# Moving the first denominator sums and the output-weight folds, and loading the last turned w_mod blocks behind wo, in a TensorE-bound attention and SwiGLU block

## The chip, the cores and the metric

The kernel runs on one core of a Trainium2 chip. The metric is the device time of one execution in microseconds; lower is better. All kernels shown here gave correct results.

"PE" is the matrix engine TensorE, "PEld" its weight loads, "DVE" VectorE, "ACT" ScalarE, "POOL" GpSimd, "SP" the engine that issues most DMA transfers.

## The reference

One block with adaptive layer norm: a linear attention, then a SwiGLU feed-forward, both gated by rows of `silu(c) @ w_mod`. Sizes: 2048 tokens, D = 1024, 32 heads of 32, F = 3584, bf16.

```python
sa, ca, ga, sb, cb, gb = split(silu(c) @ w_mod)           # six rows of 1024
h = layernorm(x) * (1 + ca) + sa
q, k, v = h @ wqkv;  pq, pk = phi(q), phi(k)              # phi(t) = t+1 if t>0 else exp(t)
kv, z = pk^T v, sum(pk)                                   # per head, over all tokens
o = (pq @ kv) / (pq . z)
x = x + ga * (o @ wo)
h = layernorm(x) * (1 + cb) + sb
x = x + gb * ((silu(h @ w_gate) * (h @ w_up)) @ w_down)
```

## The kernel before

The tokens go through in four quarters (`sc` = 0 to 3) of 512. For each quarter the kernel computes K, then V; the KV sums of a quarter (`kv_phase`) are put between the first two K groups of the next quarter and the other six. After the last quarter come the queries of the other three quarters (those of the first are done earlier), 8 groups a quarter, with small work between the groups: two transposes, the denominator sums of the first quarter (`den_sum(0)`), and four "folds", which multiply ga * wo by the KV matrix of each head so that attention and output projection become one product. `hT` is the normed input of a quarter, transposed by DMA. The rows for the gates and norms need blocks of w_mod that are also transposed while they are loaded: these are the "turned w_mod blocks" (tiles `wmt`).

```python
    def kv_phase(sc):                        # 128 weight loads and 128 matmuls, 128x32 array tiles
        kvp = acc_b("kvp", (HG, 2, DH))
        for hg in range(HG):
            for t in range(STC):
                for i in range(HPC):
                    mm(kvp[i * DH:(i + 1) * DH, hg, :, :], lhsT=pks[sc][...], rhs=v_ones(vs[sc], ...), ...)
        ...
    for sc in range(NSC):
        if sc > 0:
            k_phase(sc, 0, 2)
            kv_phase(sc - 1)
            if sc == NSC - 1:
                wo = [big("wo", [4, D]) for _ in range(2)]
                for h in range(2):
                    for g in range(4):       # eight loads of 256 KB
                        with tc.issue_after(last_load[0].ins):
                            nc.sync.dma_start(out=wo[h][g * DH:(g + 1) * DH, :, :], in_=wo_v[h, g])
            k_phase(sc, 2, 8)
        v_phase(sc)
        ...                                  # layer norm of the next quarter, DVE sums for ga, sb, cb
        if sc + 1 < NSC:                     # two transposing loads of w_mod for a later row
            with tc.issue_after(last_load[0].ins):
                last_load[0] = mod_load(*((2, gaT), (3, sbT), (4, cbT))[sc])
    ...
    q_phase(1, 2, 4)
    tpk = acc_b("tp", (2, P), BF16)
    ...                                      # two transposes of KV
    den_sum(0)                               # 32 matmuls, 128x32 tiles; one acc_b bank
    den_spread(0)
    def fold_wo(h, nb):                      # 16 matmuls, 32x32 tiles; all four acc_b banks
        ps = [acc_b("wf") for _ in range(4)]
        ...                                  # then two casts on ACT, two on DVE
    q_phase(1, 4, 6)
    fold_wo(0, 0)
    q_phase(1, 6, 8)
    fold_wo(0, 1)
    q_phase(2, 0, 2)
    fold_wo(1, 0)
    q_phase(2, 2, 3)
    fold_wo(1, 1)
    ...
    q_phase(2, 3, 4)
    den_apply(0)                             # four DVE products
    q_phase(2, 4, 6)
    for st in range(STC):
        wo_tile(st)                          # output projection of the first quarter
```

`issue_after` only fixes the order in which one engine issues; it adds no wait.

## Time and profile before

| | kernel before |
|---|---|
| time, median of 6 runs | 834.01 us (833.39 to 834.51) |
| span in the trace | 831.7 us |
| granted TensorE clock | 1.0 |

Two lines of the page: busy time of each engine with its share of the span, and the chain of waits that ended last.

```profile
PE 820.7 (99%) x4502; PEld 379.3 (46%) x4581; DVE 344.8 (41%) x655; ACT 168.7 (20%) x253; POOL 64.4 (8%) x166
PE 98%; DVE 1%; issue 1%; ACT 0%; POOL 0%
```

Only TensorE counts: it is 98% of that chain. How long a piece costs it is best read on ScalarE: every query group ends in an exp, and nearly every exp starts when its group is finished (of ScalarE's 74.8 us of idle time before the 64 exps of K and query groups, 70.5 us ended with a matmul). This is the timeline of ScalarE in the kernel before (start, duration, instruction, and in brackets the idle time before it and what ended it).

```profile
146.99 0.60 ACT L295 ACTIVATE eb<-acc 128x512 bf16<-128x512 f32 x1 [1.14 <-DVE wo L557]
...
153.43 0.60 ACT L295 ACTIVATE eb<-acc 128x512 bf16<-128x512 f32 x1 [1.13 <-PE acc L98]
155.93 0.60 ACT L295 ACTIVATE eb<-acc 128x512 bf16<-128x512 f32 x1 [1.91 <-PE acc L98]
157.66 0.60 ACT L295 ACTIVATE eb<-acc 128x512 bf16<-128x512 f32 x1 [1.13 <-PE acc L98]
159.86 0.60 ACT L295 ACTIVATE eb<-acc 128x512 bf16<-128x512 f32 x1 [0.64 <-PE acc L98]
...
167.70 0.60 ACT L295 ACTIVATE eb<-acc 128x512 bf16<-128x512 f32 x1 [0.63 <-PE acc L98]
...
170.70 0.60 ACT L295 ACTIVATE eb<-acc 128x512 bf16<-128x512 f32 x1 [0.73 <-PE acc L98]
...
174.15 0.60 ACT L295 ACTIVATE eb<-acc 128x512 bf16<-128x512 f32 x1 [1.13 <-DVE pq L459]
```

A plain group is 1.73 us (155.93 to 157.66). Transposes and sums added 0.77 us (153.43 to 155.93), fold 1 0.47 us (157.66 to 159.86), but fold 4 added 1.27 us (167.70 to 170.70). The chain of waits says why (start, duration, what):

```profile
166.46 0.69 DVE pq L298
167.16 1.20 DVE wo L596 x2
168.36 0.04 issue
168.40 0.43 PE wf L98 x13
```

Fold 4 waited for VectorE to empty the banks of fold 3, only one query group earlier.

And the DMA queue's timeline there, first the turned w_mod blocks, then wo:

```profile
110.76 8.85 SPq L388 DMA_TRANSPOSE wmt<-in_w_mod_dram  x2
119.70 4.89 SPq L544 DMA_DIRECT2D wo<-in_A_wo_dram  x8
```

### The profile page before, as it was taken

How to read it: one execution, taken by the hardware profiler on the slowest of the kernel's cores; microseconds unless marked ns; L12 is line 12 of the kernel's file. 1: busy time of each engine (PE TensorE's matmuls, PEld its weight loads, DVE VectorE, ACT ScalarE, POOL GpSimd, SP SyncE). 2: the span in 40 equal slices, each digit the busy share in tenths (PEclk: the TensorE clock that was granted, in tenths of full speed). 3: DMA queues.
4: the chain of work that ended last, by engine and by line, in shares of the span. 5: the costliest groups of instructions: out<-in, count | busy, mean ns of one | idle time of the engine just before them, and what ended most of it. 6: DMA issues, size and time to landing. Idle time of an engine off the chain costs nothing.

```text
span 831.7 us, 11105 instructions
## 1 busy us (share of the span) xinstructions
PE 820.7 (99%) x4502; PEld 379.3 (46%) x4581; DVE 344.8 (41%) x655; ACT 168.7 (20%) x253; POOL 64.4 (8%) x166
## 2 busy tenths in 40 slices
PE   8999999999999999999999999999999999999998
PEld 4444444444444444444444444444444444444444
DVE  5757779896344335421111354211114431111122
ACT  3445343434111111101111110111111101111000
POOL 2101020110221101100000010000001100000000
PEclk9999999999999999999999999999999999999999
DMA  9793694229996635646343173753405529610011
GB/s 328 292 203 90 119 214 88 53 81 280 377 239 230 216 126 165 169 142 218 116 140 114 54 219 95 250 193 98 156 1 169 154 69 346 228 47 0 19 58 51
DMA packets 144100, 129.07 MB, mean 155 GB/s; under 512 B 58608, under 2 KB 124656, under 8 KB 143536
## 3 DMA queue, kind: packets, MB, share of 16 engines
q1 hardware_dynamic: 139968, 114.97, 46.5%
q0 software_dynamic: 3792, 12.98, 5.2%
q8 instruction: 36, 0.59, 0.3%
q10 hardware_dynamic: 288, 0.40, 0.1%
q14 instruction: 16, 0.13, 0.0%
HBM read 101.98 MB, written 12.72 MB: 138 GB/s over the span
## 4 chain that ended last, share of the span: by engine, by line
PE 98%; DVE 1%; issue 1%; ACT 0%; POOL 0%
PE acc L98 90%; PE a_ps L98 7%; PE kvp L98 1%; DVE stats L224 0%; PE mod_ps L98 0%; PE den L98 0%; ACT xn L234 0%; DVE wo L596 0%; PE tp L101 0%; PE wf L98 0%; DVE pq L298 0%; ACT eb L295 0%; POOL rstd L218 0%; DVE mv L225 0%; DVE veps L216 0%
## 5 line engine op out<-in xcount | busy, mean ns | idle before, releaser
L98 PE MATMUL acc<-h2T,wgu 128*128 128x512 bf16 x1756 | 385.7, 379 | 1.9
L98 PEld LDWEIGHTS <-wgu 128*128 128x128 bf16 x1792 | 175.3, 98 | 211.3
L665 DVE TENSOR_TENSOR gu<-acc,e 128x512 bf16<-128x512 f32 x112 | 77.4, 691 | 289.9 <-PE acc L98 278.8
L98 PE MATMUL acc<-wd,gu 128*128 128x512 bf16 (+2 forms) x908 | 195.2, 372 | 0.9
L664 ACT ACTIVATE e<-acc 128x512 f32<-128x512 f32 x112 | 66.9, 597 | 374.8 <-PE acc L98 363.4
L98 PEld LDWEIGHTS <-gu 128*128 128x128 bf16 x924 | 89.3, 98 | 104.5
L98 PEld LDWEIGHTS <-hT 128*128 128x128 bf16 x512 | 49.6, 98 | 59.9 <-issue 0.7
L686 DVE TENSOR_TENSOR e<-acc,gb_bc 128x512 f32<-128x512 f32 (+2 forms) x33 | 22.3, 675 | 131.7 <-PE acc L98 122.7
L98 PE MATMUL a_ps<-wo,pq 128*128 128x512 bf16 x250 | 56.9, 379 | 0.3
L98 PE MATMUL acc<-wk,hT 128*128 128x512 bf16 x251 | 56.3, 379 | 0.7 <-issue 0.5
L98 PE MATMUL acc<-hT,wq 128*128 128x512 bf16 x248 | 55.7, 379 | 0.8 <-issue 0.6
L98 PE MATMUL acc<-wv,hT 128*128 128x512 bf16 x249 | 55.5, 379 | 0.4
L295 ACT ACTIVATE eb<-acc 128x512 bf16<-128x512 f32 x64 | 37.9, 596 | 74.8 <-PE acc L98 70.5
L234 ACT ACTIVATE xn<-x,nmr,rstd 128x1024 bf16<-128x1024 f32 x16 | 19.8, 1240 | 126.0 <-POOL nmr L232 126.0
L633 POOL DMA_DIRECT2D x_scratch<-x x16 | 9.8, 615 | 378.2 <-DVE x L626 378.2
L98 PEld LDWEIGHTS <-pq 128*128 128x128 bf16 x256 | 25.1, 98 | 30.2
L98 PEld LDWEIGHTS <-wq 128*128 128x128 bf16 x256 | 24.6, 98 | 29.8 <-issue 0.9
L296 DVE TENSOR_SCALAR eb<-eb 128x512 bf16<-128x512 bf16 x64 | 18.4, 291 | 32.2 <-ACT eb L295 32.0
L218 POOL TENSOR_TENSOR rstd<-veps,neg_half 128x1 f32<-128x1 f32 x32 | 17.8, 556 | 102.5 <-DVE veps L216 90.9
L626 DVE TENSOR_TENSOR x<-a_ps,x_sb 128x512 f32<-128x512 f32 x32 | 22.1, 690 | 8.1 <-PE a_ps L98 7.4
L689 DVE TENSOR_TENSOR ob<-e,x1r 128x512 bf16<-128x512 f32 (+2 forms) x33 | 22.3, 675 | 1.0
L627 DVE BATCH_NORM_STATS2 stats<-x 128x6 f32<-128x512 f32 x32 | 22.2, 694 | 1.1
(88 smaller groups left out, 297.3 us busy)
## 6 DMA issues: line engine op xcount, KB each, us to landing
wgu<-in_B_w_gate_dram SPq DMA_DIRECT2D x28, 1024.0 KB, 7.9
wgu<-in_B_w_up_dram SPq DMA_DIRECT2D x28, 1024.0 KB, 8.3
x_sb<-in_A_x_dram SPq DMA_DIRECT2D x32, 256.0 KB, 5.8
x_scratch<-x POOLq DMA_DIRECT2D x16, 512.0 KB, 3.4
x1r<-x_scratch SPq DMA_DIRECT2D x31, 256.0 KB, 2.8
wd<-in_B_w_down_dram SPq DMA_DIRECT2D x7, 1024.0 KB, 6.2
rbc<-rden_scratch POOLq DMA_DIRECT2D x16, 256.0 KB, 7.3
out_dram<-ob SPq DMA_DIRECT2D x31, 128.0 KB, 1.7
```

What stands on the lines that cost most here:

```text
L98: return tc.keep_in_program_order(nc.tensor.matmul(out, lhsT=lhsT, rhs=rhs, start=start, stop=stop))
L218: nc.gpsimd.tensor_tensor(out=rstd[:, 0:n], in0=veps[:, 0:n], in1=neg_half[:].to_broadcast([P, n]), op=ALU.pow)
L234: nc.scalar.activation(out=dst, in_=src, func=ACT.Identity, bias=nmr[:], scale=rstd[:, 0:1])
L295: nc.scalar.activation(out=e[:], in_=acc, func=ACT.Exp)
L296: nc.vector.tensor_scalar(out=e[:], in0=e[:], scalar1=1.0, scalar2=PHI_EPS, op0=ALU.min, op1=ALU.add)
L626: nc.vector.tensor_tensor(out=x1[:, ns], in0=a_ps[:], in1=x_t[:, ns], op=ALU.add)
L627: nc.vector.bn_stats(out=stats[:, nb, :], in_=x1[:, ns])
L633: nc.gpsimd.dma_start(out=x1_dram[st * P:(st + 1) * P, :], in_=x1[:])
L664: nc.scalar.activation(out=sg[:], in_=ps[0][:], func=ACT.Silu)
L665: gm = nc.vector.tensor_tensor(out=guT[sc][f // GPT][:, f % GPT, :], in0=ps[1][:], in1=sg[:], op=ALU.mult)
L686: nc.vector.tensor_tensor(out=yt, in0=y_ps, in1=gb_bc[:, ns], op=ALU.mult)
L689: nc.vector.tensor_tensor(out=ob, in0=yt, in1=x1r, op=ALU.add)
```

## The change

It takes away the wait of fold 4 by keeping all folds two query groups apart, joins the denominator sums to fold 1 so that TensorE leaves its full-array shape once less, and puts wo ahead of the last turned w_mod blocks in the DMA queue. Cut to its core:

```diff
-    def den_sum(sc):
+    def den_sum(sc, den=None):
-        den = acc_b("den")
+        den = den or acc_b("den")
 ...                                            # in the loop over quarters, sc == NSC - 1
-                            nc.sync.dma_start(out=wo[h][...], in_=wo_v[h, g])
+                            last_load[0] = nc.sync.dma_start(out=wo[h][...], in_=wo_v[h, g])
+                with tc.issue_after(last_load[0].ins):
+                    mod_load(4, cbT)
             k_phase(sc, 2, 8)
 ...
-        if sc + 1 < NSC:
+        if sc + 2 < NSC:
             with tc.issue_after(last_load[0].ins):
-                last_load[0] = mod_load(*((2, gaT), (3, sbT), (4, cbT))[sc])
+                mod_load(*((2, gaT), (3, sbT))[sc])
 ...
     q_phase(1, 2, 4)
     ...                                        # two transposes
-    den_sum(0)
-    den_spread(0)
-    q_phase(1, 4, 6)
-    fold_wo(0, 0)
-    q_phase(1, 6, 8)
-    fold_wo(0, 1)
-    q_phase(2, 0, 2)
-    fold_wo(1, 0)
-    q_phase(2, 2, 3)
-    fold_wo(1, 1)
+    q_phase(1, 4, 5)
+    den_sum(0, acc_a())
+    fold_wo(0, 0)
+    den_spread(0)
+    q_phase(1, 5, 7)
+    fold_wo(0, 1)
+    q_phase(1, 7, 8)
+    q_phase(2, 0, 1)
+    fold_wo(1, 0)
+    q_phase(2, 1, 3)
+    fold_wo(1, 1)
 ...
-        den_apply(0)
-    q_phase(2, 4, 6)
+        applied = den_apply(0)
+    with tc.issue_after(applied.ins):
+        q_phase(2, 4, 6)
```

More of the change, by code (lines that the diff above doesn't have):

```diff
@@ L458, in den_apply @@
             ks = slice(2 * k, 2 * k + 2)
-            nc.vector.tensor_tensor(out=pq[:, ks, :], in0=pq[:, ks, :], in1=rbc[:, ks, :], op=ALU.mult)
+            last = nc.vector.tensor_tensor(out=pq[:, ks, :], in0=pq[:, ks, :], in1=rbc[:, ks, :], op=ALU.mult)
+        return last
     nc.vector.memset(sel[:], 0.0)
@@ L543 @@
                         with tc.issue_after(last_load[0].ins):
-                            nc.sync.dma_start(out=wo[h][g * DH:(g + 1) * DH, :, :], in_=wo_v[h, g])
+                            last_load[0] = nc.sync.dma_start(out=wo[h][g * DH:(g + 1) * DH, :, :], in_=wo_v[h, g])
+                with tc.issue_after(last_load[0].ins):
+                    mod_load(4, cbT)
             k_phase(sc, 2, 8)
@@ L578 @@
                             in1=zmask[:], op=ALU.mult)
-    q_phase(1, 2, 4)
-    tpk = acc_b("tp", (2, P), BF16)
-    for h in range(2):
-        transpose(tpk[:, h, :], KVB[:, 4 * h:4 * h + 4, :].rearrange("p g e -> p (g e)"))
-    nc.vector.tensor_copy(out=KVT, in_=tpk[:])
-    den_sum(0)
-    den_spread(0)
     def fold_wo(h, nb):
@@ L596, in fold_wo @@
             (nc.scalar.copy if g % 2 == 0 else nc.vector.tensor_copy)(out=wo[h][:, g, ns], in_=ps[g][:])
-    q_phase(1, 4, 6)
+    q_phase(1, 2, 4)
+    tpk = acc_b("tp", (2, P), BF16)
+    for h in range(2):
+        transpose(tpk[:, h, :], KVB[:, 4 * h:4 * h + 4, :].rearrange("p g e -> p (g e)"))
+    nc.vector.tensor_copy(out=KVT, in_=tpk[:])
+    q_phase(1, 4, 5)
+    den_sum(0, acc_a())
     fold_wo(0, 0)
-    q_phase(1, 6, 8)
+    den_spread(0)
+    q_phase(1, 5, 7)
     fold_wo(0, 1)
-    q_phase(2, 0, 2)
+    q_phase(1, 7, 8)
+    q_phase(2, 0, 1)
     fold_wo(1, 0)
-    q_phase(2, 2, 3)
+    q_phase(2, 1, 3)
     fold_wo(1, 1)
```

## The prediction

> **What bounds the kernel.** TensorE. On the page PE is busy 820.7 of 831.7 us (99%) at full granted clock, and the chain of waits is 98% PE. PE's waits sum to about 4 us, nearly all before 25 us. So only PE time around the moved work can be won. I take the real pace from the starts of the exp on ScalarE (timeline of ACT), each of which waits for one finished query group: a plain group of 8 matmuls advances them by 1.73 us.
>
> **What the moved pieces cost PE now** (from one exp to the next, less 1.73 us):
> - two transposes and den_sum(0): 153.43 to 155.93, 0.77 us; the transposes are 0.11 of it in the chain, so the sums 0.66.
> - folds 1 to 3: 0.47, 0.47, 0.46 us.
> - fold 4: 167.70 to 170.70, 1.27 us, 0.80 more. The chain shows why: it comes one query group after fold 3, and its fourth matmul needs a PSUM bank that a VectorE cast of fold 3 frees at 168.36; three matmuls had begun at 167.6. The wait table shows only 0.23 us of it, since matmul ends are modelled.
>
> **Removed.** Folds 1 to 2 and 2 to 3 are two groups apart already and show no stall, so the 0.80 us should go. Sums joined to fold 1: three later sums together cost 1.55 us (between two VectorE gate products, 5.01 instead of 3.46); one alone costs 0.66. So a sum is about 0.44, and leaving the full array and coming back about 0.2. One such excursion disappears, but the sums (128x32) and the fold (32x32) still differ in tile shape. [...] Estimate: 0.15 us gained (0 to 0.25).
>
> **Added.** No new computing. VectorE gets the sums' two operations (0.28 + 0.95 us) just before the casts of fold 1. My estimate: these casts end 3.3 us after fold 1; fold 2 comes 3.5 us after it. That is tight: if a phi (0.98 us) goes between the casts, fold 2 waits 0.3 to 0.7 us.
>
> **Moved, off the path.**
> - den_sum(0) ends about 1.9 us later, so the broadcast denominators land at about 170 instead of 168 us. den_apply(0) follows the phi of query group (2,3): now 172.26, then about 171.3. Still 1 us of slack; VectorE's order (apply, then two phi) is already this one, so the new ordering edge should change nothing.
> - wo loads before the last turned w_mod blocks: wo is scaled at 142 to 147 and needed at 157; the turned blocks are used from 135. Both have slack. Risk: wo's transfers now run beside the last transposes into hT (landing 113.8; PE starts on that hT at 115.65).
>
> **Sum.** 833.55 - 0.80 - 0.15 = 832.6 us. Range 831.9 to 833.5. Faster by over 2%: 0.5%; within 2%: 99%; slower: 0.5%.
>
> **What would show it.** Folds 2 to 4 each step the exps by 0.47 us and no cast stands in the chain of waits; sums plus fold 1 cost about 1.0 us instead of 1.13; the last exp before the output projection (now 174.15) starts about 0.95 us earlier, and all after it keeps that lead to the end. den_apply starts straight after a phi, without idle time for a DMA.
>
> **What would make it wrong.** A stall at fold 2 behind the reciprocal (gain 0.3 to 0.5); a late hT transpose or late denominators stalling PE (loss of up to 1 us); instruction order elsewhere changed by the scheduler, showing in the gate stage; run noise, 1.1 us between the three runs.

The sum: 833.55 - 0.80 - 0.15 = 832.6 us, where the 0.15 us is my estimate from the 0.66 and 1.55 us above.

## More of the kernel before

One more stretch matters later, the chain of waits around the KV phase of the third quarter. "Issue" is time for which the profile shows nothing that was waited for.

```profile
117.97 1.29 PE acc L98 x6
119.27 1.30 PE kvp L98 x128
120.56 0.16 issue
120.72 1.24 PE acc L98 x5
121.96 0.21 issue
122.17 4.92 PE acc L98 x22
```

The 0.21 us at 121.96 looks like nothing.

## The result, and the profile after

| | before | after |
|---|---|---|
| median of 6 runs | 834.01 us (833.39 to 834.51) | 837.21 us (835.58 to 838.26) |
| span in the trace | 831.7 us | 833.7 us |
| last exp before the output projection | 174.15 us | 176.12 us |

The ratio is 1.0037, 95% interval 1.0025 to 1.005. A ratio here is the mean time of one kernel's runs over the mean of the other's of the same rounds, so not quite the ratio of the medians. The change made the kernel slower by 0.4%; 832.6 had been predicted. All outputs are right.

The page of the changed kernel has the same busy time in a longer span:

```profile
PE 820.4 (98%) x4502; PEld 379.3 (46%) x4581; DVE 344.3 (41%) x655; ACT 168.7 (20%) x253; POOL 64.6 (8%) x166
```

ScalarE's timeline answers to the lines of before:

```profile
149.86 0.60 ACT L295 ACTIVATE eb<-acc 128x512 bf16<-128x512 f32 x1 [1.14 <-DVE wo L560]
...
156.30 0.60 ACT L295 ACTIVATE eb<-acc 128x512 bf16<-128x512 f32 x1 [1.13 <-PE acc L98]
158.14 0.60 ACT L295 ACTIVATE eb<-acc 128x512 bf16<-128x512 f32 x1 [1.24 <-PE acc L98]
...
160.90 0.60 ACT L295 ACTIVATE eb<-acc 128x512 bf16<-128x512 f32 x1 [0.71 <-PE acc L98]
162.63 0.60 ACT L295 ACTIVATE eb<-acc 128x512 bf16<-128x512 f32 x1 [1.13 <-PE acc L98]
...
164.82 0.60 ACT L295 ACTIVATE eb<-acc 128x512 bf16<-128x512 f32 x1 [0.63 <-PE acc L98]
...
170.47 0.60 ACT L295 ACTIVATE eb<-acc 128x512 bf16<-128x512 f32 x1 [1.13 <-PE acc L98]
...
172.67 0.60 ACT L295 ACTIVATE eb<-acc 128x512 bf16<-128x512 f32 x1 [0.63 <-PE acc L98]
...
176.12 0.60 ACT L295 ACTIVATE eb<-acc 128x512 bf16<-128x512 f32 x1 [1.13 <-DVE pq L459]
```

Nearly everything that the prediction said of this stretch holds. Transposes alone add 0.11 us (156.30 to 158.14), sums and fold 1 together 1.03 us (to 160.90), fold 2 0.46 us, fold 4 0.47 us. From the first exp of the second quarter's queries to the last before the projection it takes 26.26 us (149.86 to 176.12) where it took 27.16 us (146.99 to 174.15): 0.90 us gained.

But that first exp comes 2.87 us later, and the whole of it is lost in one place. The chain of waits around the KV phase of the third quarter is now:

```profile
119.26 1.15 PE kvp L98 x128
120.41 0.16 issue
120.57 1.24 PE acc L98 x5
121.81 3.23 issue
125.05 2.12 PE acc L98 x9
```

The 0.21 us of before has become 3.23 us, still without anything that the profile could name.

Two things about these "issue" pieces matter. The pieces of 0.16 us behind a change of tile shape are not waits: the first matmul there is missing from the record. In `half_held` (experiment 5), whose trace has all 4581 matmuls instead of 4502, that matmul is there and the piece is gone: the chain goes on at 120.42 us without it. The other two are real, and larger than they look, since the ends of matmuls are modelled. By the exps, from the last before the KV phase to the first behind it, an undisturbed pass takes 2.98 us (119.31 to 122.29 in `half_held`). It took 3.51 us before (119.30 to 122.82) and takes 6.39 us now (to 125.69): 0.53 us lost before, 3.41 us now.

The DMA queue's timeline has the new order:

```profile
110.81 3.84 SPq L545 DMA_DIRECT2D wo<-in_A_wo_dram  x8
114.75 17.64 SPq L388 DMA_TRANSPOSE wmt<-in_w_mod_dram  x2
```

The trace also keeps one record for each DMA packet, those of the instruction queues too. 36 packets of 16,384 bytes run in an execution, on a queue of their own (q8); in the gate stage of the kernel before they are 27.4 us apart on average (25.0 to 30.1), about the time of 128 matmuls with 128 weight loads (128 x 1.73 / 8 = 27.7 us). The page counts 4502 + 4581 recorded PE and PEld instructions, some matmuls missing; `half_held`, with the same work for TensorE, has 4581 of each, 9162, and 36 blocks of 256 are 9216. By these counts they are TensorE's instructions, 256 in a block; experiment 2 puts that to the test. The packet that matters stands in the DMA view for 119 to 121 us of the kernel before, and for 122 to 124 us of the changed one (queue, packets, MB, share of 16 engines' time):

```profile
q8 instruction: 1, 0.02, 3.5%
```

```profile
q8 instruction: 1, 0.02, 4.2%
```

Their records give it from 119.78 to 120.90 us before, and from 122.41 to 123.75 us after. In both TensorE goes on about 1.3 us behind its end (122.17 and 125.05).

That makes the theory. A KV phase is 128 weight loads and 128 matmuls in 1.15 us: it eats a whole block of instructions, which takes about 27.4 us in the gate stage. By this theory the block behind it must come within a few microseconds, and in the changed kernel its fetch waits for wo's 2 MB, whose last packet ended at 122.29 us, 0.12 us before the block's began. The rivals: the moves of the sums and folds cost something that this one trace hides; TensorE waits for data; or it is the turned blocks, now issued from 114.75 us, that hold the fetch.

### The profile page after: what moved, and what is told of

Read it like the earlier page. It is cut to its first block, busy times and chain, and to the rows that moved or that the text cites. A ratio compares the mean times of both kernels' runs of the same rounds, so it can differ in the third digit from the quotient of the medians.

```text
span 833.7 us, 11103 instructions
## 1 busy us (share of the span) xinstructions
PE 820.4 (98%) x4502; PEld 379.3 (46%) x4581; DVE 344.3 (41%) x655; ACT 168.7 (20%) x253; POOL 64.6 (8%) x166
## 4 chain that ended last, share of the span: by engine, by line
PE 98%; issue 1%; DVE 1%; ACT 0%; POOL 0%
PE acc L98 90%; PE a_ps L98 7%; PE kvp L98 1%; DVE stats L224 0%; PE mod_ps L98 0%; PE wf L98 0%; PE den L98 0%; ACT xn L234 0%; PE tp L101 0%; POOL rstd L218 0%; DVE mv L225 0%; DVE veps L216 0%; DVE e L689 0%; DVE sc L489 0%; DVE ob L692 0%
## 5 line engine op out<-in xcount | busy, mean ns | idle before, releaser
L334 ACT CAST v<-acc 128x512 bf16<-128x512 f32 x32 | 18.3, 581 | 21.3 <-PE acc L98 20.6
```

Of the source, the lines that this page charges most:

```text
L334: nc.scalar.copy(out=v[:, t * D + nb * NB:t * D + (nb + 1) * NB], in_=acc[:])
```

## The experiments

"Gap" below is the longest "issue" piece near 122 us in the chain of waits of the run's trace. The medians of the kernel before, in the same jobs, are given with each.

### 1. Only the moves, and only the loads

`old_load_order` is the changed kernel with the loads in their old order:

```diff
-                            last_load[0] = nc.sync.dma_start(out=wo[h][...], in_=wo_v[h, g])
-                with tc.issue_after(last_load[0].ins):
-                    mod_load(4, cbT)
+                            nc.sync.dma_start(out=wo[h][...], in_=wo_v[h, g])
 ...
-        if sc + 2 < NSC:
+        if sc + 1 < NSC:
-                mod_load(*((2, gaT), (3, sbT))[sc])
+                last_load[0] = mod_load(*((2, gaT), (3, sbT), (4, cbT))[sc])
```

> The changed kernel with the loads in their old order (last turned w_mod blocks first, wo behind them); all TensorE moves kept. Theory (the loss is one late fetch of TensorE's next instruction block, held back by wo's transfers; the moves of the sums and folds gain 0.9 us): the TensorE gap at about 122 us shrinks from 3.2 to 0.2 us as in the kernel before, the instruction packet starts near 119.8 us, time about 0.9 us under the kernel before (833.1). Rival (the moves of sums and folds cost something later, or in other runs): time stays near 837.

Measured: 833.51 us (833.40 to 833.85; kernel before 833.65), ratio 1.000 (0.9988 to 1.0013). The loss is gone, but the 0.9 us did not show either. Its trace has the gap at 0.71 us, the packet starting at 120.54 us, and 0.5 us lost before 25 us, where TensorE waited longer for w_mod. By the exps its KV phase took 4.01 us, 0.50 more than in the trace of the kernel before, which alone eats half of the 0.9 us. Experiment 8 takes this up.

`only_load_order` is the reverse, the kernel before with the same edit in the other direction.

> The kernel before with only the loads in the new order. Theory: TensorE gap of 3 us or more at about 122 us, the instruction packet starting after wo's transfers end (about 122.4), and 3 to 4 us more than the kernel before (837 to 838). Rival (the order of loads is harmless, the moves on TensorE cost): within 0.3 us of the kernel before.

Measured: 837.74 us (836.39 to 838.95; before 833.65), ratio 1.0051 (1.0038 to 1.0065). Gap 3.32 us, packet at 122.53 us:

```profile
121.83 3.32 issue
```

The order of the loads alone makes the whole loss, and more than the whole. The first rival has fallen.

### 2. The blocks shifted by 72 instructions

`shift_new` leaves the loads in their new order and moves the whole instruction stream of TensorE against its block boundaries:

```diff
         mod_rows_a(2)
-        keep_warm(spare, 5)
+        keep_warm(spare, 1)
+        for _ in range(40):
+            mm(spare[:, 0:1], lhsT=sel[:, 0, :], rhs=sel[:, 0, 0:1], start=True, stop=True)
```

`keep_warm` issues matmuls whose results nobody reads, here before 14 us. Each matmul is two instructions, its weight load and itself (4581 of each in the trace of `half_held`).

> The changed kernel, loads in the new order, with 72 more TensorE instructions before 14 us: four 512-column warming matmuls are replaced by 40 of one column, about the same time. The 16 KB boundaries of TensorE's instruction stream then no longer coincide with the ends of the KV phases. Theory (late instruction block, urgent only because the KV phase eats 256 instructions, a whole block, in 1.2 us): no gap at 122 us although wo's transfers still run there; about 1.0 us under the kernel before. Rival (TensorE waits at 122 us for data, a buffer or a DMA of its operands): gap of 3 us stays.

Measured: 832.35 us (832.20 to 832.57; before 833.65), ratio 0.9985 (0.9973 to 0.9998). There is no gap, though wo's transfers run from 112 to 123 us as in the changed kernel:

```profile
119.51 1.15 PE kvp L98 x128
120.67 0.16 issue
120.83 6.21 PE acc L98 x28
```

The block that was late is now fetched at 109.85 us, before wo is issued (111.99 us). The data, buffers and loads are the same; only the place of the block boundary differs. So TensorE had waited for instructions, and a wait for data is ruled out. This version beats both kernels, and by more than the 0.9 us of the moves, since the 0.53 us that the kernel before lost at this boundary is gone too.

### 3. Which transfers hold the fetch

`mod_held` keeps the turned blocks out of the time in question. A small write on VectorE to their tiles, behind the phi of the fourth K group, makes their loads wait (none of them is issued from 118 to 130 us in its trace):

```diff
             t = big("wmt", [DC // 2, D])
+            if hold:
+                with tc.issue_after(last_phi[0].ins):
+                    nc.vector.memset(t[:, 0, 0:1], 0.0)
 ...
-                    mod_load(4, cbT)
-            k_phase(sc, 2, 8)
+            k_phase(sc, 2, 4)
+            if sc == NSC - 1:
+                with tc.issue_after(last_load[0].ins):
+                    mod_load(4, cbT, hold=True)
+            k_phase(sc, 4, 8)
```

> The changed kernel, but the turned w_mod blocks are held back until the phi of the fourth K group of the last quarter (a small VectorE write to their tiles), so that at 111 to 122 us only wo's transfers run. If wo's transfers hold the instruction fetch: gap of about 3 us at 122 us stays, as in the changed kernel. If the turned blocks queued behind wo (issued from 114.75 us) hold it: gap gone or 0.2 us.

Measured: 837.50 us (837.28 to 837.73; before 833.65), ratio 1.0047 (1.0033 to 1.0061). Gap 3.00 us, packet at 121.97 us:

```profile
121.81 3.00 issue
```

It is wo's transfers; the turned blocks behind them are innocent.

This trace also showed a second loss. The table by stretches (time, then busy time of PE, PEld, DVE, ACT, POOL, granted clock, DMA share, GB/s) right after the gap:

```profile
121.60:124.90 3.30, 0.30 (x2) 0.09 (x2) 0.03 (x1) 0.00 (x0) 0.00 (x0) 1.00 0.15 25
124.90:128.80 3.90, 3.90 (x11) 1.44 (x12) 2.12 (x4) 0.66 (x2) 0.72 (x2) 0.57 0.32 71
128.80:132.00 3.20, 3.20 (x16) 1.45 (x15) 1.72 (x4) 1.13 (x2) 0.00 (x0) 0.99 0.00 0
```

The clock is halved for 3.41 us (125.43 to 128.85 in its record), and the work between the exps at 125.46 and 135.78 us takes 10.32 us, where it took 8.63 us in the changed kernel's trace (125.69 to 134.32): 1.69 us more. What makes the clock fall is not shown, and the length of a gap does not decide it alone: behind the 3.00 us here it fell; in the trace of the changed kernel it stayed through 3.23 us (mean clock 1.0, 835.58 us), and in that of `only_load_order` through 3.32 us (granted clock 1.00 in each stretch from 112 to 140 us). The five other runs of the changed kernel show a lower mean clock (0.996 to 0.998, 836.83 to 838.26 us). Where in them it fell is not recorded, but the size fits: an estimate, 0.002 x 835 us = 1.7 us, against the 1.6 us between the profiled run and the median.

### 4. A shift of only 16 instructions

`shift_small` is `shift_new` with one warming matmul replaced by nine of one column.

```diff
-        keep_warm(spare, 5)
+        keep_warm(spare, 4)
+        for _ in range(9):
+            mm(spare[:, 0:1], lhsT=sel[:, 0, :], rhs=sel[:, 0, 0:1], start=True, stop=True)
```

> The changed kernel with the blocks shifted by only 16 instructions (one warming matmul replaced by nine of one column). Theory: the fetch is asked for 8 matmul pairs (1.7 us) earlier while the end of the block comes only 0.07 us earlier, so the gap at about 122 us falls from 3.2 to about 1.5 us, and moves 16 instructions (8 matmuls) forward, into the end of the KV phase or just behind it. Rival (the fetch starts when wo's transfers end, whenever it was asked for): the packet still starts near 122.4 us and the gap stays at 3 us or more.

Measured: 839.01 us (837.70 to 840.05; before 833.60), ratio 1.0063 (1.005 to 1.0077). My number was wrong, the rival's right.

```profile
119.49 1.14 PE kvp L98 x126
120.62 4.43 issue
125.06 0.24 PE kvp L98 x2
```

The gap did move forward by eight pairs of weight load and matmul, from six weight loads behind the KV phase to two matmuls before its end, which confirms the block boundary. But the packet started at 122.40 us, as if asked for at the same time: asking earlier gained nothing, and the fetch started when wo's transfers were through (1024 of 1024 packets). By the estimate of the next section it was asked for at about 114.4 us, when seven of wo's eight loads had been issued (the eighth at 114.45 us); whether the eighth was ahead of it is not shown. That the asking has a fixed place in the instruction stream, as the expectation has it, was my assumption: no record shows it (its 1.7 us is an estimate, 8 x 1.73 / 8, and so is its 0.07 us, 16/256 of 1.15). The fixed delay after the asking that I had assumed does not fit. The clock was halved here for 6.83 us (123.08 to 129.91 us in its record; granted clock 0.50 in the stretch from 125.1 to 129.9 us), which comes on top of the longer gap.

### 5. Half of wo held back

`half_held` tests this from the other side: only four of wo's eight loads are issued before the fetch; the other four, and the turned blocks behind them, are issued from 121.43 us.

```diff
                 wo = [big("wo", [4, D]) for _ in range(2)]
+                with tc.issue_after(last_phi[0].ins):
+                    nc.vector.memset(wo[1][:, 0, 0:1], 0.0)
```

> The changed kernel, but the second half of wo is held back until the phi of the second K group of the last quarter (about 121 us), the turned w_mod blocks behind it. wo's first half then transfers alone at 111 to 116 us. Theory: the instruction packet, asked for at about 116 us, starts before 119.5 us and the gap is under 0.3 us; time 832.3 to 833.3. Rival (anything of the new order but the traffic at 116 to 122 us): gap of about 3 us.

Measured: 832.28 us (832.00 to 832.50; before 833.60), ratio 0.9983 (0.997 to 0.9997). No gap:

```profile
119.27 1.15 PE kvp L98 x128
120.42 5.72 PE acc L98 x26
```

The packet starts at 117.40 us. Counted in the packet records, it follows wo's data in each of the five runs that have wo ahead:

| run | wo issued ahead of the fetch | wo packets of 2 KB through at its start | start, us | gap, us |
|---|---|---|---|---|
| changed kernel | 8 loads, 110.8 to 114.6 | 1024 of 1024 | 122.41 | 3.23 |
| only_load_order | 8 loads | 1024 of 1024 | 122.53 | 3.32 |
| mod_held | 8 loads | 1014 of 1024 | 121.97 | 3.00 |
| shift_small | 8 loads | 1024 of 1024 | 122.40 | 4.43 |
| half_held | 4 loads, 110.8 to 112.8 | 511 of 512 | 117.40 | none |
| kernel before | none | none | 119.78 | 0.21 |

When the fetch was asked for is not in the trace; "about 116 us" in the expectation is an estimate. At the fourth KV phase (148.6 us in the kernel before) the packet of the same place starts 3.3 us ahead of the phase, at 145.30 us, and is the only DMA packet between 143 and 147 us; an estimate from this puts the asking for the third at about 115.9 us, after the last wo load has been issued. In the kernel before, the turned blocks are issued ahead of it and its packet, at 119.78 us, is late too. It did not wait for all of them: 6,774 of their 8,192 packets of 256 bytes were through when it started. So that the fetch waits for what was issued ahead of it is shown for wo alone, down to the last few packets (1014 to 1024 of 1024, 511 of 512).

### 6. The same shift for the other kernels

`shift_old` is `shift_new` with the loads in their old order, `shift_before` the kernel before with the same shift; their edits are those of 1 and 2.

> The changed kernel with the loads in their old order and the TensorE instruction blocks shifted by 72 instructions. Theory: with no urgent block fetch the order of the loads is worth nothing, so the same as the shifted changed kernel (832.35), within 0.3 us. Rival (the old order of loads loses something of its own, as its 833.51 in place of the expected 833.1 might say): 0.5 us or more above the shifted changed kernel.

Measured: 832.72 us (832.23 to 833.63; before 833.60), ratio 0.999 (0.9978 to 1.0003). With the boundary out of the way the order of loads makes about 0.4 us of the medians (832.72 against 832.35, two jobs), and the ranges overlap. This is 0.07 us outside what I had expected, and short of the rival's 0.5.

> The kernel before with the blocks shifted by 72 instructions. Theory: the small gap of the kernel before (0.2 us in its trace) has the same cause and varies from run to run; it goes, the spread of the runs falls from 1.6 to about 0.4 us, and the time is 0.9 us above the shifted changed kernel: about 833.25. Rival (the shift itself, not the fetch, made the changed kernel faster): over 1 us under the kernel before.

Measured: 833.76 us (833.10 to 834.20; before 833.60), ratio 1.000 (0.9986 to 1.0013). A miss: the gap near 122 us is gone from its trace, but the spread stays. Its trace shows another small loss, of 0.46 us: the last transposes into hT came late (VectorE waited 1.9 us for them, `shift_new` 1.0), and TensorE's first K group of the last quarter ran at the pace of VectorE, weight loads 0.32 us apart instead of 0.22. So the run-to-run spread of the kernel before is not the block's gap alone.

### 7. What the moves on TensorE gain

With the shift the gap is gone (the longest "issue" wait in these three traces is 0.2 us), so three kernels of one job can be compared. `shift_only_load` is the kernel before with the new order of loads and the shift. `shift_folds` has in addition the folds in their new places, while `den_sum(0)` stays alone behind the transposes. `shift_half` is the changed kernel with both cures.

> The kernel before with only the loads in the new order, and the instruction blocks shifted by 72 instructions: the late block does no harm, so this against the shifted changed kernel (832.35) measures what the moves on TensorE gain. Theory: 0.9 us more, about 833.25, spread of the runs 0.5 us or less. Rival (the gain of 0.9 us seen between 150 and 176 us is given back later): 832.4.

> As the run before it, with the folds two query groups apart, but the denominator sums still alone behind the transposes. Theory: the folds' distance is worth 0.80 us, joining sums and fold 0.10 us: about 832.45, and every fold steps the exps by 0.47 us. Rival (joining matters more than spacing): 832.8 or more.

> The changed kernel with both cures, blocks shifted by 72 instructions and the second half of wo held back. Theory: either cure alone already removes the gap, so no gain over them: 832.0 to 832.4.

Measured, with 834.30 us for the kernel before: 833.32 us (833.01 to 833.99), 832.43 us (832.08 to 833.60) and 832.28 us (832.08 to 833.46); ratios 0.999 (0.9978 to 1.0003), 0.9981 (0.9967 to 0.9994) and 0.9981 (0.9968 to 0.9993). Spacing the folds is worth 0.80 us in the traces, where fold 4 steps the exps by 0.47 us instead of 1.27. In the medians it is 0.89 us, but the ranges overlap, and the spread of the first kernel is twice the 0.5 us that I had expected. Joining the sums is worth 0.10 us in the traces (1.03 us for sums and fold 1 together; in `shift_folds` 0.66 and 0.47). The two cures together show no gain over one (832.35 and 832.28 us, in other jobs). The spread of `shift_folds` is again late hT: its profiled run, the 833.02, lost about 0.8 us to weight loads 0.32 us apart at 86 to 89 us (its third KV phase begins at 119.98 us, that of `shift_half` at 119.18).

### 8. The old order once more

`old_again` is the program of `old_load_order`, for a second trace.

> The changed kernel with the loads in their old order, the same program as in the first run of this study, for a second trace. That run missed its 0.9 us: its trace had lost 0.5 us before 25 us (TensorE waiting for w_mod) and 0.5 us more than the kernel before at the block gap (LDWEIGHTS 1.30 us apart instead of 0.80). If both are chance of a run, this trace shows other values of them, and its last exp before the output projection starts at 173.25 us plus whatever it loses there beyond the kernel before; if they belong to the program, both come again.

Measured: one run, 833.13 us (kernel before 834.05), span 831.4 us, and the exp at 173.75 us. The 0.5 us before 25 us did not come again, so they look like chance. The gap came again, 0.72 us, with the packet at 120.11 us. With 174.15 - 0.90 + 0.51 = 173.76 the sum closes. By the exps the KV phase took 4.02 us here and 4.01 us in the first trace, against 3.51 us in the one trace of the kernel before. Whether this half microsecond belongs to the program or to that one trace stays open; up to 122 us the two programs should be alike.

## Why the prediction was wrong

- "TensorE is the bound": right, in both kernels.
- "The 0.80 us should go": right. Fold 4 steps the exps by 0.47 us and no cast stands in the chain.
- "Estimate: 0.15 us gained (0 to 0.25)" for joining sums and fold: measured 0.10 us. Why it is not more is not shown.
- "If a phi goes between the casts, fold 2 waits": it did not. Both casts of fold 1 ran at 160.89 to 162.11, ahead of the phi.
- "den_apply starts straight after a phi": right, at 174.23 us, when the phi that began at 173.63 us was done. The new ordering edge changed nothing there.
- "wo loads before the last turned w_mod blocks: ... Both have slack": this step failed. It is true of the data: wo and the turned blocks came in time. I asked only who reads what a transfer brings. TensorE's instructions come by DMA too (36 packets of 16,384 bytes on q8); one of their blocks had about no slack, since the KV phase uses up 256 instructions in 1.15 us, and I put 2 MB in front of it: its packet started at 122.41 us instead of 119.78. Cost: 2.87 us in the trace, and an estimated 1.6 us more in the median, which the lower clock of the other runs fits. The risk that I named, late transposes into hT, was the right kind of thought at the wrong victim.
- The prediction put PE's 4 us of waits "nearly all before 25 us". That was not so: its wait table has 1.2 us of "issue" in seven pieces, all behind 90 us. Six of them are the missing records of 0.16 us; the seventh was the warning.
- The trace of before had shown it: 0.21 us of "issue" at 121.96 us, 0.53 us by the exps, behind the only kind of phase in which TensorE issues 256 instructions in about a microsecond. I had filed it under waits too small to matter. A short wait can be the tip of one with no slack left.
- The range was too narrow for this: it allowed a loss of up to 1 us against the forecast, and thought of nothing before 150 us but a late hT.

The best versions are the changed kernel with half of wo held back (832.28 us, 1.3 us under the kernel before in its job) or with its blocks shifted (832.35 us, also 1.3 us).

## What to carry to other kernels

Before moving a large load earlier, ask not only who needs its data but what else is moved by DMA while it runs. Here that included the instructions of the engine that bounds the kernel, and a stretch of 256 tiny instructions in 1.15 us made the next instruction block urgent: 2 MB ahead of it cost 3.23 us of waiting. Where a kernel has such a stretch, look for a short "issue" wait just behind it, keep large loads out of the few microseconds ahead of it, or move the block boundary with a few cheap instructions; here the first gave 832.28 us and a shift of 72 instructions 832.35, while one of 16 made it 839.01. When only the time is asked, such a loss looks like the fault of the edit one has been thinking about; running each half of the change alone separates them at once.
